# A four-layer transformer kernel rebuilt as one list-scheduled pipeline over token tiles, with the attention scores in packs of four 32-row matmuls

## The chip, the cores and the metric

One core of one Trainium2 chip. The metric is the device time of one execution in microseconds (us). The kernel before takes 821.77 us (median of 3 runs, 820.84 to 821.87). Engines are named as in the profile: PE (TensorE), PEld (its weight loads), DVE (VectorE), ACT (ScalarE), POOL (GpSimd), SP (DMA issue).

The records of TensorE's granted clock show two levels, full and half. The profile gives the mean of the granted clock; this document turns it into "half-clock time" = 2 x (1 - mean clock) x span, the time at half rate that gives that mean. For the kernel before this is 2 x (1 - 0.933) x 818.5 = 110 us. The spacing of matmuls agrees with the records: 512-column matmuls of one stream start every 216 ns where the record says full and every 426 ns where it says half.

## The reference, cut to what matters

S = 2048 tokens, D = 512, 32 heads of 16, a causal window of 256, an MLP of width 1792, bf16. Two layer kinds, each applied twice:

```python
def _A_ref(x, wqkv, wo):                       # H = 32; Dh = 16; W = 256
    q, k, v = ...                              # x @ wqkv, split into heads
    scores = einsum("bhqd,bhkd->bhqk", q, k) * Dh ** -0.5
    mask = (i - j >= 0) & (i - j < W)          # three 128-key blocks per 128 queries
    p = softmax(where(mask, scores, -1e9))
    return einsum("bhqk,bhkd->bhqd", p, v) (heads joined) @ wo

def _B_ref(x, w1, b1, w2, b2):
    return gelu(x @ w1 + b1) @ w2 + b2

x = x + _A_ref(layernorm(x), A_wqkv, A_wo)
x = x + _B_ref(layernorm(x), B_w1, B_b1, B_w2, B_b2)
x = x + _A_ref(layernorm(x), A_wqkv, A_wo)
x = x + _B_ref(layernorm(x), B_w1, B_b1, B_w2, B_b2)
```

The window makes a token tile depend only on itself and the two tiles before it, in every layer. So the four layers can be run as one stream over tiles; nothing forces a layer to end before the next begins.

## The kernel before

It runs layer by layer. `layer_A` normalises all 16 tiles and makes Q, K and V for all of them, then runs attention over 16 tiles; `layer_B` normalises all tiles, then runs the MLP by groups of four tiles. Each `op` goes to its engine's in-order queue in the order in which it is written.

A head has only 16 of the 128 rows of the contraction. The kernel expands K: for each head a copy of 128 rows of K with all rows but that head's 16 set to zero, so that a plain 128-row matmul gives one head's scores.

```python
# K expansion, per tile four multiplies of 128x1024 on VectorE (L614)
op("dve", lambda e, ...: e.tensor_tensor(
    out=KTb[:, sb, kc * HC : (kc + 1) * HC, :],
    in0=KT[:, kc, kcols][:, None, :].to_broadcast([P, HC, P]),
    in1=headmask[:, :, None].to_broadcast([P, HC, P]), op=ALU.mult), ...)

# scores: one 128-row matmul for each head and tile (L638)
op("pe", lambda e, ...: e.matmul(sc[:, ps, hi, 0:N], KTb[:, sb, h, :], QT[:, kc, qcols],
                                 start=True, stop=True), ...)

# exp of two heads (L689); both edges of the band in one VectorE multiply for four heads (L659)
op("act", lambda e, ...: e.activation(Eband[:, eb, h0 : h1 + 1, 0:N], sc[:, ps, :, 0:N], AF.Exp, scale=SCALE), ...)
op("dve", lambda e, ...: e.tensor_tensor(out=Eband[...][:, :, 0:3:2, :], in0=Eband[...][:, :, 0:3:2, :],
                                         in1=mask01[:, None, :, :].to_broadcast([P, nh, 2, P]), op=ALU.mult), ...)

# PV (L710): per head up to three 17-column matmuls (16 values and a sum); then reciprocal,
# normalisation, transposes, output projection, residual, one tile behind
...
# the order of one attention layer
PVLAG = 3
for i, (t, p) in enumerate(jobs):              # tile, pair of heads
    if p in ktb_at: emit_ktb(t + 1, [ktb_at[p]])
    emit_scores(t, p); emit_exp(t, p)
    if p % MASKGRP == MASKGRP - 1: emit_mask(t, p - MASKGRP + 1, p)
    if i >= PVLAG: emit_pv(*jobs[i - PVLAG])
    ...                                        # norm, transposes, output projection of tile t-1
```

LayerNorm's normalisation, its square root and the copies of Q and K out of PSUM run on ScalarE. GpSimd does almost nothing.

The softmax here doesn't subtract the row's maximum and nothing guards it: scores larger than these inputs give would overflow.

## Time and profile before

| | before |
|---|---|
| time, median | 821.77 us |
| span of the profiled execution, mean granted clock | 818.5 us, 0.933 |
| PE / ACT / DVE / POOL busy | 664 / 562 / 471 / 9 us |
| attention, two stretches | 212 + 216 us for 32 tiles: 13.4 us a tile |
| LayerNorm and QKV stretches, four | 68 + 45 + 58 + 46 = 217 us |
| MLP stretches, two | 85 + 89 us |

The page's busy times (share of the span, instructions):

```profile
span 818.5 us, 13174 instructions
...
PE 664.2 (81%) x5728; PEld 362.7 (44%) x5728; DVE 470.9 (58%) x769; ACT 561.6 (69%) x814; POOL 9.3 (1%) x30
```

No engine is full on average. The next view says why: the span in 40 slices, each digit the busy share of a slice in tenths; the last line is the granted clock.

```profile
PE   4996778777778649999979877778787775699998
DVE  5428888888888670222323488887878786401111
ACT  5757888888888476444357488888888884753330
PEclk9998998999999658999989999999999997599999
```

Four stages stand side by side, and twice: where PE is at 9, DVE and ACT are at 1 to 4 (the MLP), and where those are at 8, PE is at 7 (attention). The clock falls in the short stretches between attention and MLP. The table of windows gives the same with numbers. Its columns are the window, its length, the busy time (and count) of PE, PEld, DVE, ACT and POOL, the mean clock, DMA share and GB/s:

```profile
core 0: us, PE busy (x) PEld busy (x) DVE busy (x) ACT busy (x) POOL busy (x), PEclk, DMA share, GB/s
...
68.00:280.00 212.00, 164.94 (x2062) 107.43 (x2063) 172.52 (x248) 179.80 (x254) 0.00 (x0) 0.94 0.01 1
280.00:325.00 45.00, 30.19 (x153) 13.90 (x150) 18.78 (x53) 29.27 (x46) 0.00 (x0) 0.66 0.00 0
325.00:410.00 85.00, 85.00 (x381) 35.74 (x380) 23.31 (x49) 36.59 (x50) 0.00 (x0) 1.00 0.00 1
410.00:468.00 58.00, 51.26 (x270) 24.38 (x268) 17.40 (x33) 36.37 (x58) 2.28 (x1) 0.94 0.00 1
...
```

In attention ACT is busy for 180 and DVE for 173 of 212 us, PE for 165; ACT and DVE wait for each other by way of PE, which is read from the chain below and was not tested. The LayerNorm stretch (280 to 325) uses no engine well and runs PE at clock 0.66. The MLP stretch is bound by PE alone: 85 of 85 us. The chain that ended last, by engine and by line ("issue" is time in which an engine waited for nothing that the profile shows, and a q behind an engine's name marks its sequencer):

```profile
PE 45%; DVE 40%; ACT 14%; issue 1%; POOL 1%; ACTq 0%; POOLq 0%
DVE L_KTb L614 18%; DVE L_Eband L659 12%; PE L_hp L846 12%; PE L_yp L887 12%; ACT L_Eband L689 10%; PE L_pjA L546 6%; PE L_sc L638 4%; PE L_pjA L569 3%; DVE stat L362 3%; PE L_oy L710 3%; DVE X L502 2%; ACT L_xn L439 2%; DVE L_OT_sb L762 1%; PE L_yp L878 1%; DVE statmv L368 1%
```

and the groups that the change touches (line, engine, operation, output and inputs, count; then busy time, mean ns of one, idle time before them and what ended it; "+2 forms" means that the mean mixes three shapes):

```profile
L689 ACT ACTIVATE L_Eband<-L_sc 128x768 bf16<-128x768 f32 (+2 forms) x512 | 363.6, 769 | 72.2 <-PE L_oy L710 61.7
...
L638 PE MATMUL L_sc<-L_QT,L_KTb 128*128 128x384 bf16 (+2 forms) x1024 | 251.7, 332 | 19.7 <-ACT L_Eband L689 10.8
...
L659 DVE TENSOR_TENSOR L_Eband<-L_Eband,mask 128x1024 bf16<-128x1024 bf16 x224 | 151.6, 687 | 64.6 <-ACT L_Eband L689 64.4
...
L614 DVE TENSOR_TENSOR L_KTb<-L_KT,headmask 128x1024 bf16<-128x1024 bf16 x128 | 155.5, 1219 | 0.1
```

The K expansion is a third of DVE's work and 18% of the chain. A score matmul's 332 ns is its length in a pipeline; when scores stand densely in the trace, one starts about every 163 ns (median).

### The profile page before, as it was taken

How to read it: one execution, taken by the hardware profiler on the slowest of the kernel's cores; microseconds unless marked ns; L12 is line 12 of the kernel's file. 1: busy time of each engine (PE TensorE's matmuls, PEld its weight loads, DVE VectorE, ACT ScalarE, POOL GpSimd, SP SyncE). 2: the span in 40 equal slices, each digit the busy share in tenths (PEclk: the TensorE clock that was granted, in tenths of full speed). 3: DMA queues.
4: the chain of work that ended last, by engine and by line, in shares of the span. 5: the costliest groups of instructions: out<-in, count | busy, mean ns of one | idle time of the engine just before them, and what ended most of it. 6: DMA issues, size and time to landing. Idle time of an engine off the chain costs nothing.

```text
span 818.5 us, 13174 instructions
## 1 busy us (share of the span) xinstructions
PE 664.2 (81%) x5728; PEld 362.7 (44%) x5728; DVE 470.9 (58%) x769; ACT 561.6 (69%) x814; POOL 9.3 (1%) x30
## 2 busy tenths in 40 slices
PE   4996778777778649999979877778787775699998
PEld 2442445454555424444435334545454553344443
DVE  5428888888888670222323488887878786401111
ACT  5757888888888476444357488888888884753330
POOL 3000000000000000000010000000000000000000
PEclk9998998999999658999989999999999997599999
DMA  9100000000000000000000000000000000000000
GB/s 339 46 1 0 2 1 2 2 2 2 1 2 1 2 0 1 1 1 1 0 2 1 0 1 2 1 2 1 2 1 2 2 1 2 0 14 19 21 20 33
DMA packets 9675, 10.80 MB, mean 13 GB/s; under 512 B 2193, under 2 KB 8594, under 8 KB 9618
## 3 DMA queue, kind: packets, MB, share of 16 engines
q1 hardware_dynamic: 9618, 9.97, 3.5%
q8 instruction: 45, 0.74, 0.3%
q14 instruction: 12, 0.10, 0.0%
HBM read 7.87 MB, written 2.10 MB: 12 GB/s over the span
## 4 chain that ended last, share of the span: by engine, by line
PE 45%; DVE 40%; ACT 14%; issue 1%; POOL 1%; ACTq 0%; POOLq 0%
DVE L_KTb L614 18%; DVE L_Eband L659 12%; PE L_hp L846 12%; PE L_yp L887 12%; ACT L_Eband L689 10%; PE L_pjA L546 6%; PE L_sc L638 4%; PE L_pjA L569 3%; DVE stat L362 3%; PE L_oy L710 3%; DVE X L502 2%; ACT L_xn L439 2%; DVE L_OT_sb L762 1%; PE L_yp L878 1%; DVE statmv L368 1%
## 5 line engine op out<-in xcount | busy, mean ns | idle before, releaser
L689 ACT ACTIVATE L_Eband<-L_sc 128x768 bf16<-128x768 f32 (+2 forms) x512 | 363.6, 769 | 72.2 <-PE L_oy L710 61.7
L638 PE MATMUL L_sc<-L_QT,L_KTb 128*128 128x384 bf16 (+2 forms) x1024 | 251.7, 332 | 19.7 <-ACT L_Eband L689 10.8
L710 PE MATMUL L_oy<-L_Vaug,L_Eband 128*128 128x17 bf16 x2880 | 180.9, 173 | 83.0 <-DVE L_Eband L659 76.3
L710 PEld LDWEIGHTS L_oy<-L_Vaug,L_Eband 128*128 128x128 bf16 x2880 | 160.3, 99 | 171.5 <-DVE L_Eband L659 99.8
L659 DVE TENSOR_TENSOR L_Eband<-L_Eband,mask 128x1024 bf16<-128x1024 bf16 x224 | 151.6, 687 | 64.6 <-ACT L_Eband L689 64.4
L614 DVE TENSOR_TENSOR L_KTb<-L_KT,headmask 128x1024 bf16<-128x1024 bf16 x128 | 155.5, 1219 | 0.1
L864 ACT ACTIVATE L_gT<-L_hp,b1T 128x512 bf16<-128x512 f32 x112 | 76.0, 687 | 87.3 <-PE L_hp L846 87.2
L502 DVE TENSOR_TENSOR X<-X,L_yp 128x512 bf16<-128x512 bf16 x32 | 22.0, 688 | 176.8 <-PE L_yp L887 176.8
L846 PE MATMUL L_hp<-L_xnT,W_sb 128*128 128x512 bf16 x448 | 105.5, 391 | 1.4 <-ACT L_xnT L474 1.4
L887 PE MATMUL L_yp<-W_sb,L_gT 128*128 128x512 bf16 x448 | 102.3, 380 | 0.0
L638 PEld LDWEIGHTS L_sc<-L_QT,L_KTb 128*128 128x128 bf16 x1024 | 69.7, 98 | 49.0 <-ACT L_Eband L689 25.8
L846 PEld LDWEIGHTS L_hp<-L_xnT,W_sb 128*128 128x128 bf16 x448 | 44.8, 100 | 57.7 <-issue 6.1
L887 PEld LDWEIGHTS L_yp<-W_sb,L_gT 128*128 128x128 bf16 x448 | 41.2, 98 | 52.6 <-issue 7.2
L546 PE MATMUL L_pjA<-L_xnT,Wqkv_sb 128*128 128x512 bf16 x256 | 58.0, 385 | 1.4 <-ACT L_QT L558 1.4
L581 DVE CAST L_Vaug<-L_pjA 128x512 bf16<-128x512 f32 x32 | 22.2, 694 | 61.0 <-PE L_pjA L569 60.8
L774 PE MATMUL L_oy<-Wo_sb,L_OT_sb 128*128 128x512 bf16 x128 | 49.3, 394 | 1.0 <-DVE L_OT_sb L762 1.0
L439 ACT ACTIVATE L_xn<-X,nbias,rstd 128x512 bf16<-128x512 bf16 x64 | 46.7, 803 | 1.8 <-DVE nbias L395 1.8
L362 DVE BATCH_NORM_STATS2 stat<-X 128x6 f32<-128x512 bf16 x64 | 43.1, 673 | 5.4 <-DMA X<-in_A_x_dram 4.8
L452 PE MATMUL L_tpB<-ident,L_xn 128*128 128x128 bf16 x128 | 19.4, 307 | 24.5 <-ACT L_xn L439 15.3
L546 PEld LDWEIGHTS L_pjA<-L_xnT,Wqkv_sb 128*128 128x128 bf16 x256 | 25.2, 100 | 31.4 <-ACT L_QT L558 1.9
L377 ACT ACTIVATE sqv<-statmv,epscol 128x4 f32<-128x4 f32 x16 | 4.8, 297 | 43.0 <-DVE statmv L368 43.0
L558 ACT ACTIVATE L_QT<-L_pjA 128x512 bf16<-128x512 f32 x32 | 18.8, 599 | 15.0 <-PE L_pjA L546 15.0
(45 smaller groups left out, 300.7 us busy)
## 6 DMA issues: line engine op xcount, KB each, us to landing
W_sb<-in_B_w_dram SPq DMA_DIRECT2D x2, 1792.0 KB, 15.4
X<-in_A_x_dram SPq DMA_DIRECT2D x4, 512.0 KB, 6.0
out_dram<-X SPq DMA_DIRECT2D x16, 128.0 KB, 1.7
Wqkv_sb<-in_A_wqkv_dram SPq DMA_DIRECT2D x1, 1536.0 KB, 10.1
Wo_sb<-in_A_wo_dram SPq DMA_DIRECT2D x1, 512.0 KB, 10.6
b1raw<-in_B_b_dram SPq DMA_DIRECT2D x1, 3.5 KB, 15.5
b2row<-in_B_b_dram SPq DMA_DIRECT2D x1, 1.0 KB
```

The costliest lines, as they stand in the source:

```text
L362: lambda e, t=t: e.bn_stats(stat6[:, t, :], X[:, t, :]),
L439: lambda e, t=t, s=s: e.activation(xn[:, s, :], X[:, t, :], AF.Identity, bias=nbias[:, t : t + 1], scale=rstd[:, t : t + 1],),
L546: lambda e, s=s, dc=dc, kc=kc, which=which, cols=cols: e.matmul(pj[:, s, :], Wqkv_sb[:, dc, which * D + kc * P : which * D + (kc + 1) * P] ...
L614: lambda e, sb=sb, kc=kc, kcols=kcols: e.tensor_tensor(out=KTb[:, sb, kc * HC : (kc + 1) * HC, :], in0=KT[:, kc, kcols][:, None, :].to_bro ...
L638: lambda e, ps=ps, hi=hi, sb=sb, h=h, kc=kc, N=N, qcols=qcols: e.matmul(sc[:, ps, hi, 0:N], KTb[:, sb, h, :], QT[:, kc, qcols], start=True ...
L659: lambda e, eb=eb, ha=ha, hb=hb, nh=nh: e.tensor_tensor(out=Eband[:, eb, ha : hb + 1, :].rearrange("p h (b q) -> p h b q", q=P)[:, :, 0:3: ...
L689: lambda e, ps=ps, h0=h0, h1=h1, eb=eb, N=N: e.activation(Eband[:, eb, h0 : h1 + 1, 0:N], sc[:, ps, :, 0:N], AF.Exp, scale=SCALE,),
L710: lambda e, m=m, half=half, col0=col0, eb_k=eb_k, h=h, blk=blk, k=k, kmin=kmin, t=t: e.matmul(oy[:, m, half, col0 : col0 + VW], Eband[:, e ...
L774: lambda e, m=m, c=c: e.matmul(oy[:, m, 1, :], OT_sb[:, c, :], Wo_sb[:, c, :], start=(c == 0), stop=(c == DC - 1)),
L846: lambda e, s=s, dc=dc, fc=fc, cols=cols: e.matmul(hp[:, s, :], W1_sb[:, dc, fc * P : (fc + 1) * P], xnT[:, dc, cols], start=(dc == 0), st ...
L864: lambda e, s=s, fc=fc, gs=gs: e.activation(gT[:, gs, fc, :], hp[:, s, :], AF.Gelu_apprx_tanh, bias=b1T[:, fc : fc + 1], scale=1.0,),
L887: lambda e, ys=ys, gs=gs, fc=fc, ti=ti: e.matmul(yp[:, ys, :], gT[:, gs, fc, ti * P : (ti + 1) * P], W2_sb[:, fc, :], start=False, stop=(f ...
```

## The change

Its intent: no stage stands alone, so that each engine always finds work of some layer; and less work for DVE and ACT in attention. In parts:

1. A planner (`_Plan`) takes every operation with an estimated duration, a priority, its reads and writes and the PSUM banks it takes, simulates the five queues and writes the order in which each engine gets its instructions. The order is fixed when the kernel is built.
2. 32 steps, 16 tiles by two repetitions. Step tau holds the attention of tile tau; QKV is made two pairs of tiles ahead, and the MLP of four tiles is put in behind the attention.
3. Scores: K is written twice when it leaves PSUM, with even heads or odd heads set to zero; a 32-row slice of such a copy holds one head. Four matmuls of 32 rows, one on each 32-row group of the array, form a pack. The K expansion goes.
4. The diagonal edge of the band is masked on DVE, the far edge by a select on GpSimd; LayerNorm's root becomes a power on GpSimd, its normalisation goes to DVE; all copies out of PSUM go to DVE. ACT is left with exp and GELU.
5. Eight PSUM banks: scores take six in rotating sets of four; two ("o") serve PV, transposes, QKV, projections and the second MLP matmul.

The diff has some 1300 lines; this is its core, with cuts marked. Line numbers in the profiles of the changed kernel are those of its own file (L504 is the matmul of `pe_group`, L582 the score pack, L593 and L596 the exps, L600 the mask, L605 the select, L625 PV).

```diff
+    PL = _Plan({"sc": [(0, 1, 2, 3), (4, 5, 0, 1), (2, 3, 4, 5)], "o": [(6,), (7,)],
+                "m1": [(5,), (6,), (7,), (4,), (3,), (2,), (1,), (0,)]})
 ...
+    dma(b1_dma, ["b1raw"], prio=-91)          # planned with the default landing time, 3.0 us
+    add("dve", lambda e, B: e.tensor_copy(b1T[:], b1raw[:]), 100, reads=["b1raw"], writes=["b1T"], prio=-50)
 ...
-    op("dve", ... KTb = KT * headmask ...)    # K expansion, 128 x 128x1024
+    for par in range(2):                      # K out of PSUM, even or odd heads
+        add("dve", lambda e, B, ...: e.tensor_scalar(out=KT[:, kb, par, 2 * i : 2 * i + 2, :],
+            in0=ps[:, B[g][0], :]..., scalar1=parmask[:, par : par + 1], scalar2=None, op0=ALU.mult), ...)
 ...
-    op("pe", ... e.matmul(sc[:, ps, hi, 0:N], KTb[:, sb, h, :], QT[:, kc, qcols]) ...)
+    def sc(e, B, c=c, par=par, gT3=gT3, gS1=gS1):
+        bk = tuple(B[gT3]) + tuple(B[gS1])
+        for r in range(RG):
+            rows = slice(32 * r, 32 * r + 32)
+            x = e.matmul(ps[:, bk[r], 0:N], KT[rows, kb, par, c, kc0 : kc0 + P],
+                         QT[rows, c, t * P : t * P + N], start=True, stop=True)
+        return x
 ...
+    add("dve", ... E[:, es, :, 0:P] *= mask01 ...)                        # diagonal edge
+    if nb == 3:
+        add("pool", lambda e, B, es=es: e.affine_select(                  # far edge
+            E[:, es, :, 2 * P : 3 * P], E[:, es, :, 2 * P : 3 * P], [[0, RG], [-1, P]],
+            ALU.is_ge, 0.0, base=-1, channel_multiplier=1), ...)
 ...
+    def mlp(J, gate_tau, prio1, prio2):
+        gate_pe = (visit_node[(gate_tau, NV - 1)],) if gate_tau < NT else ()
+        gate_act = (exp_last[gate_tau],) if gate_tau < NT else ()
+        for fc in range(FC):
+            pe_group(g, [... W1 ...], 512, 1, xr + ["W1"], prio1 + fc * 0.1, cls="m1", after=gate_pe)
+            gelu_last[0] = add("act", ... Gelu_apprx_tanh ..., after=gate_act)
+        for i in range(4):
+            pe_group(g, [... b2, W2 ...], 512, 1, ..., prio2 + i)
+            residual(tau, 1, g, prio2 + i)
 ...
+    # in attention(): the first exp of a step waits for the last GELU so far
+    if v == 0 and gelu_last[0] is not None:
+        aft = (gelu_last[0],)
 ...
+    qkv(0, -40)
+    qkv(1, -30)
+    for tau in range(NT + BLAG + 1):
+        base = 100.0 * tau
+        if tau % 2 == 0 and tau + 4 < NT:
+            qkv(tau // 2 + 2, base + 120)
+        if tau < NT:
+            attention(tau, base)
+            outproj(tau, base + 130)
+        if tau >= 3 + BLAG and (tau - 3 - BLAG) % 4 == 0:
+            J = (tau - 3 - BLAG) // 4
+            mlp(J, tau, base + 95, base + 250)
```

## The prediction

> **What bounds the kernel now.** It runs four separated stages (timeline, span 818.5 us): LayerNorm+QKV 0-68, attention 68-280, LayerNorm+MLP 280-410, then the same again to 819. PE is busy 664 us, ACT 562, DVE 471 (page), and each stage has its own limit. In attention (2 x about 214 us) ACT is busy 180 of 212 us: the chain of waits gives 40% to DVE (18% K expansion, 12% masking), and ACT waits 62 us in front of exps. In MLP (2 x about 105 us) PE is full at 216 ns per 512-column matmul and ACT and DVE are mostly idle; in the 45 us LayerNorm stretches PE is mostly idle at clock 0.66-0.70.
>
> **What changes.** The main gain is the first.
> - All layers become one pipeline over 32 tile steps, so MLP and QKV matmuls fill PE's gaps under exp.
> - K expansion (128 x 1219 ns, 155 us DVE) goes. PSUM copy with parity mask replaces QK copies: 64 x about 0.7 = 45 us, plus Q copies 22 us, now on DVE instead of ACT.
> - Scores: four K=32 tiles side by side. Before, 1024 matmuls, about 160 ns each when dense (165 us); after, 256 packs. The Trainium skill, "TensorE: Matmul & The Clock Gate", section "Measured speedup vs the span model", gives 3.07x for four row tiles of 512 columns. The skill ("TensorEngine Tiling (Array Packing)", "Key Properties") says a mode change drains PE; estimate 0.4 us per pack with both changes, 100 us.
> - ACT loses normalisation, square roots and all copies (about 110 us). Remaining: exp 364, GELU 76, 16 table loads 20: 460 us.
> - DVE, from measured durations: diagonal masks 256 x 0.42 = 108, stats 55, 64 normalisations about 20, transposed copies 27, K/Q/V 90, reciprocals 256 x about 0.19 = 49, small multiplies 256 x about 0.22 = 56, output copies 13, residuals 44: about 460 us.
> - POOL: 224 selects of 512 elements, from 292 ns for 128: about 0.6 us each, 135 us, plus 128 tiny ops.
> - PE dense: 1184 matmuls of 512 columns 256 us, 512 of 256 columns 56, transposes 22, 2880 PV at about 28 ns (six in 0.16 us in the timeline) 81, scores 100: about 515 us.
>
> **Sum.** Three nearly balanced engines: PE 515, ACT 460, DVE 460. ACT is idle in part of each of 8 GELU phases (56 matmuls 12.1 us, 14 GELUs 9.5). Only two PSUM banks serve PV, projections, transposes and W2; I estimate 12.7 us of holding per step before queueing, against 16.1 of PE. Static order, semaphore latency and these banks should keep the busiest engine near 85%: about 600 us steady, plus about 14 us start and about 20 us end (last MLP alone). Prediction **630 us**, range **575 to 700**. Chances: faster by over 2% 0.96, within 2% 0.02, slower 0.02.
>
> **What would show each step.** Stages gone in the timeline, ACT and DVE busy evenly to the last 25-30 us; ACT about 460, DVE about 460-490, POOL 150-180; PE clock above 0.95; K-expansion group absent; a score pack start to next start 0.3-0.45 us; no engine above about 85% and short waits spread over PE, ACT and DVE, many at PSUM buffers freed by DVE.
>
> **What would make it wrong.** Score packs not overlapping (+70 us PE). POOL selects slowed by DVE masks sharing its SBUF interface ("GPSIMD Engine Reference", "Specifications"; no POOL work overlaps here before), delaying PV. The two PSUM banks queueing worse than thought (towards 700). Small PSUM operations on DVE above 0.2 us.

## The result, and the profile after

The changed kernel is correct and takes **694.28 us** (median of 4 runs, 691.72 to 696.11), beside 821.82 us (820.84 to 822.86) for the kernel before on the same chip. The ratio is 0.8446, with a 95% interval of 0.8416 to 0.8475. Ratios here are the mean time of one kernel's fast runs over that of the other's of the same rounds, so not quite the ratio of the medians quoted. (The first median given for the kernel before is of three of the same four runs.) The prediction was 630 us with a range of 575 to 700: the direction is right, the time lies inside the range but 64 us above the middle.

The page's busy times, then the 40 slices:

```profile
span 694.4 us, 14552 instructions
...
PE 581.8 (84%) x5984; PEld 298.2 (43%) x5984; DVE 423.9 (61%) x1249; ACT 451.9 (65%) x640; POOL 217.4 (31%) x381
```

```profile
PE   0277888898889898899978898898989898799878
...
DVE  0399788837683767838485677837486574625511
ACT  0008798788388836786187955779488964877340
...
PEclk9998687999999888997989999899999998688989
```

The stages are gone from PE's line: 7 to 9 throughout, after two slices of a slow start. But ACT and DVE still dip again and again, ACT to as low as 1. The clock is below full in more places than before, not fewer: 0.906 in the mean, 131 us at half clock against 110.

The windows of start, steady part and tail (columns as before):

```profile
core 0: us, PE busy (x) PEld busy (x) DVE busy (x) ACT busy (x) POOL busy (x), PEclk, DMA share, GB/s
0.00:50.00 50.00, 14.53 (x104) 9.26 (x104) 21.62 (x52) 1.28 (x1) 12.96 (x49) 1.00 0.49 158
50.00:655.00 605.00, 536.45 (x5709) 275.45 (x5708) 394.40 (x1177) 439.05 (x623) 203.62 (x330) 0.90 0.01 4
655.00:694.40 39.40, 30.86 (x176) 13.47 (x176) 7.85 (x22) 11.53 (x17) 0.79 (x2) 0.91 0.05 17
```

This table holds most of the miss. The prediction had 14 us of start, 600 steady and 20 of tail; measured are 50, 605 and 39.4. The chain:

```profile
PE 56%; DVE 27%; ACT 9%; issue 5%; POOL 2%; POOLq 0%; DVEq 0%
PE ps L504 44%; DVE E L600 6%; PE ps L625 5%; ACT E L593 5%; PE ps L582 5%; DVE KT L540 5%; DVE X L513 4%; ACT E L596 3%; DVE stat L470 3%; DVE xn L480 2%; DVE Va L553 2%; DVE Otm L639 2%; PE ps L488 2%; DVE R L636 1%; DVE QT L532 1%
```

and the groups:

```profile
L593 ACT ACTIVATE E<-ps 128x768 bf16<-128x768 f32 (+2 forms) x256 | 198.8, 777 | 197.0 <-PE ps L582 195.2
...
L605 POOL TENSOR_SCALAR_AFFINE_SELECT E<-E 128x512 bf16<-128x512 bf16 x224 | 161.6, 722 | 264.2 <-ACT E L596 263.8
L600 DVE TENSOR_TENSOR E<-E,mask 128x512 bf16<-128x512 bf16 x256 | 123.4, 484 | 20.6 <-ACT E L596 19.7
...
L582 PE MATMUL ps<-QT,KT 32*128 32x384 bf16 (+2 forms) x1024 | 92.3, 350 | 20.3 <-ACT E L593 19.1
```

The K expansion is gone from the chain, and the projections, QKV and MLP (all L504) are now 44% of it. ACT sat idle for 195 us in front of exps, for want of a score pack; before, exps waited 72 us in all. 48 us of that is the start; where most of the rest comes from, windows by step show (a step runs here from one tile's first score pack to the next tile's). The first is a step of attention, QKV and projection alone, the second a burst of the first MLP matmul with its GELUs, the third a step with the second MLP matmul in it:

```profile
105.60:118.70 13.10, 11.21 (x165) 6.12 (x164) 10.94 (x37) 10.96 (x16) 6.62 (x10) 0.70 0.00 1
133.00:147.20 14.20, 14.15 (x104) 6.86 (x104) 3.84 (x11) 11.62 (x16) 0.86 (x1) 0.96 0.00 1
160.90:185.60 24.70, 22.72 (x212) 10.61 (x212) 14.88 (x44) 12.38 (x17) 9.87 (x19) 0.93 0.00 1
```

Eighteen steps without an MLP burst (two of them hold 14 and 17 matmuls of W2) take 13.5 us in the mean (11.9 to 14.9). This is the 13.4 us that one attention tile took before, but it now holds its tile's LayerNorms, QKV and output projection too. Thirteen steps with a burst of W1 or W2 take 26.5 us. So the LayerNorm and QKV stretches were absorbed, and the MLP was not: it stands between steps almost as it stood between layers. The timeline of a W2 burst, PE and then ACT (start, length, operation, count, and in brackets the idle time before it):

```profile
172.98 3.31 PE L504 MATMUL ps<-W_sb,gT 128*128 128x512 bf16 x10
...
179.99 3.20 PE L504 MATMUL ps<-W_sb,gT 128*128 128x512 bf16 x14
183.02 0.45 PE L625 MATMUL ps<-Va,E 128*128 128x17 bf16 x12
183.40 0.34 PE L582 MATMUL ps<-QT,KT 32*128 32x384 bf16 x4
```

```profile
171.61 0.81 ACT L596 ACTIVATE E<-ps 128x768 bf16<-128x768 f32 x1
183.80 0.81 ACT L593 ACTIVATE E<-ps 128x768 bf16<-128x768 f32 x1 [11.38 <-PE ps L582]
```

Ten us of matmuls without one score pack among them, and ACT idle for 11.38 us. W1 bursts are like it, but there the code asks for it: W1 waits for the step's last score pack, GELU for its last exp, and the next step's first exp for the last GELU. Both orders stand in the static queues and could have been read before the run.

The start. The first row is from DVE's queue, the second from PE's:

```profile
27.12 0.17 DVE L460 CAST b1T<-b1raw 128x14 f32<-128x14 bf16 x1 [22.97 <-DMA b1raw<-in_B_b_dram]
...
28.95 0.29 PE L488 MATMUL ps<-ident,xn 128*128 128x128 bf16 x1 [28.95 <-DVE xn L480]
```

A cast of 14 columns, needed only by the first GELU, about 100 us later (the second of the three windows above), stood early in DVE's queue because the planner took its load to land after 3 us. All of LayerNorm after its first instruction stood behind it for 23 us. The Trainium skill ("TensorE: Matmul & The Clock Gate", section "Architectural detail: the array is 16× 32×32, not 1× 128×128") calls the queues of ACT and DVE strictly first-in-first-out, and this trace agrees.

The tail, on PE, after the last score pack at 654.7:

```profile
663.00 0.61 PE L488 MATMUL ps<-ident,xn 128*128 128x128 bf16 x4 [3.21 <-DVE xn L480]
664.12 13.41 PE L504 MATMUL ps<-xnTB,W_sb 128*128 128x512 bf16 x56 [0.52 <-DVE xnTB L493]
```

It is the last tile's PV, projection and LayerNorm (to 664.1), then W1 (13.4 us) and W2 (to 691.3) of the last group with nothing left to run beside them.

### The profile page after: what moved, and what is told of

Same layout as the page of the kernel before. It is cut to its first block, busy times and chain, and to the rows that moved or that the text cites. A ratio compares the mean times of both kernels' runs of the same rounds, so it can differ in the third digit from the quotient of the medians.

```text
span 694.4 us, 14552 instructions
## 1 busy us (share of the span) xinstructions
PE 581.8 (84%) x5984; PEld 298.2 (43%) x5984; DVE 423.9 (61%) x1249; ACT 451.9 (65%) x640; POOL 217.4 (31%) x381
## 4 chain that ended last, share of the span: by engine, by line
PE 56%; DVE 27%; ACT 9%; issue 5%; POOL 2%; POOLq 0%; DVEq 0%
PE ps L504 44%; DVE E L600 6%; PE ps L625 5%; ACT E L593 5%; PE ps L582 5%; DVE KT L540 5%; DVE X L513 4%; ACT E L596 3%; DVE stat L470 3%; DVE xn L480 2%; DVE Va L553 2%; DVE Otm L639 2%; PE ps L488 2%; DVE R L636 1%; DVE QT L532 1%
## 5 line engine op out<-in xcount | busy, mean ns | idle before, releaser
L593 ACT ACTIVATE E<-ps 128x768 bf16<-128x768 f32 (+2 forms) x256 | 198.8, 777 | 197.0 <-PE ps L582 195.2
L605 POOL TENSOR_SCALAR_AFFINE_SELECT E<-E 128x512 bf16<-128x512 bf16 x224 | 161.6, 722 | 264.2 <-ACT E L596 263.8
L596 ACT ACTIVATE E<-ps 128x768 bf16<-128x768 f32 (+2 forms) x256 | 199.0, 777 | 0.0
L625 PE MATMUL ps<-Va,E 128*128 128x17 bf16 x2880 | 112.4, 173 | 32.1 <-DVE Otm L639 7.7
L600 DVE TENSOR_TENSOR E<-E,mask 128x512 bf16<-128x512 bf16 x256 | 123.4, 484 | 20.6 <-ACT E L596 19.7
L625 PEld LDWEIGHTS ps<-Va,E 128*128 128x128 bf16 x2880 | 95.0, 98 | 86.5 <-issue 30.3
L504 PE MATMUL ps<-W_sb,gT 128*128 128x512 bf16 x448 | 113.8, 396 | 0.0
L582 PE MATMUL ps<-QT,KT 32*128 32x384 bf16 (+2 forms) x1024 | 92.3, 350 | 20.3 <-ACT E L593 19.1
L504 PE MATMUL ps<-xnTB,W_sb 128*128 128x512 bf16 x448 | 104.2, 388 | 0.5 <-DVE xnTB L493 0.5
L684 ACT ACTIVATE gT<-ps,b1T 128x512 bf16<-128x512 f32 x112 | 76.4, 687 | 28.4 <-PE ps L504 28.0
L504 PE MATMUL ps<-xnTA,Wqkv_sb 128*128 128x256 bf16 x512 | 84.3, 311 | 7.4 <-DVE KT L540 4.9
L474 POOL TENSOR_SCALAR veps<-statmv 128x1 f32<-128x1 f32 x64 | 14.9, 233 | 174.4 <-DVE statmv L472 174.0
L504 PEld LDWEIGHTS ps<-xnTB,W_sb 128*128 128x128 bf16 x448 | 42.9, 99 | 50.0 <-issue 3.5
L504 PEld LDWEIGHTS ps<-W_sb,gT 128*128 128x128 bf16 x448 | 40.9, 100 | 53.4 <-issue 15.4
L504 PEld LDWEIGHTS ps<-xnTA,Wqkv_sb 128*128 128x128 bf16 x512 | 49.2, 108 | 26.7 <-DVE KT L540 7.1
L663 DVE COPY OT<-ps 128x512 bf16<-128x512 bf16 x32 | 13.4, 419 | 73.9 <-PE ps L658 73.3
L582 PEld LDWEIGHTS ps<-QT,KT 32*128 32x128 bf16 x1024 | 26.3, 93 | 74.4 <-ACT E L593 46.7
L636 DVE RECIPROCAL R<-ps 128x4 f32<-128x4 f32 x256 | 44.6, 174 | 14.6 <-PE ps L625 13.6
L540 DVE TENSOR_SCALAR KT<-ps,parmask 128x512 bf16<-128x512 f32 x64 | 46.3, 738 | 4.4 <-PE ps L504 4.1
```

What stands on the lines that cost most here:

```text
L504: r = e.matmul(ps[:, B[g][0], cols], lhsT, rhs, start=st, stop=sp)
L540: kn = (add("dve", lambda e, B, g=g, i=i, par=par: e.tensor_scalar(out=KT[:, kb, par, 2 * i : 2 * i + 2, :], in0=ps[:, B[g][0], :].rearran ...
L582: x = e.matmul(ps[:, bk[r], 0:N], KT[rows, kb, par, c, kc0 : kc0 + P], QT[rows, c, t * P : t * P + N], start=True, stop=True)
L593: a = add("act", lambda e, B, gT3=gT3, es=es: e.activation(E[:, es, 0:2, 0:N], ps[:, B[gT3][0] : B[gT3][0] + 2, 0:N], AF.Exp, scale=SCALE) ...
L596: a2 = add("act", lambda e, B, gS1=gS1, es=es: e.activation(E[:, es, 2:4, 0:N], ps[:, B[gS1][0] : B[gS1][0] + 2, 0:N], AF.Exp, scale=SCALE ...
L600: add("dve", lambda e, B, es=es: e.tensor_tensor(out=E[:, es, :, 0:P], in0=E[:, es, :, 0:P], in1=mask01[:, None, :].to_broadcast([P, RG, P ...
```

## The experiments

Letters in the expectations name theories, which each text states. "Correct" is against the reference; three kernels are wrong. Three of the kernels had one run each that was slow (the fifth, seventh and ninth); ratios leave it out, the medians in the table do not.

| kernel | median us | ratio to before | half-clock us (profiled run) |
|---|---|---|---|
| changed | 694.28 | 0.8446 | 131 |
| e1_b1_late | 679.35 | 0.8265 | 141 |
| e2_w2_spread | 673.74 | 0.8215 | 106 |
| e3_staged | 719.73 | 0.8771 | 208 |
| e4_filler | 685.87 | 0.8347 | 64 |
| e5_b1_last | 669.80 | 0.8126 | 103 |
| e6_full_rows | 714.54 | 0.8699 | 10 |
| e7_no_select | 670.76 | 0.8136 | 113 (slow run) |
| e8_combined | 656.35 | 0.7991 | 140 |
| e9_select_aside | 688.94 | 0.8373 | 107 |
| e10_dve_masks | 723.66 | 0.8816 | 226 |
| e11_comb_filler | 645.91 | 0.7853 | 47 |
| e12_third_bank | 702.63 | 0.8562 | 147 |

Where a difference to the changed kernel is given in us below, it is the difference of the medians of fast runs (for the three kernels with a slow run these are 668.33, 669.98 and 687.12 us); the changed kernel was measured in another session, so the ratios, each taken beside the same kernel before, are the sounder comparison.

### The start: e1_b1_late and e5_b1_last

```diff
-        add("dve", lambda e, B: e.tensor_copy(b1T[:], b1raw[:]), 100, reads=["b1raw"], writes=["b1T"], prio=-50)
+        add("dve", lambda e, B: e.tensor_copy(b1T[:], b1raw[:]), 100, reads=["b1raw"], writes=["b1T"], prio=200)
```

> One edit: the cast of the MLP bias b1 gets a late place in VectorE's order instead of the second. Theory H: in the changed kernel VectorE sits 23.0 us at the start in front of this cast, for the last but one of the input DMAs, and everything behind it in the queue waits too; the first score pack should then start near 28 us instead of 49.9, nothing else should move, and the time fall by about 21 us, to 668 to 678 us. Rival: the start is held by the input DMAs of the weights as such (the DMA queues are busy to about 27 us); then the first score pack stays past 40 us and the time falls by less than 8 us.

Correct, 679.35 us (677.91 to 679.78). The first score pack came at 37.6 us instead of 49.9, and 15 us were gained, not the 21 expected. The trace says why: a wait of 10.16 us for the same load remained. The planner fills an idle queue with whatever it holds ready, so a lower priority moved the cast only a little. The edit was not strong enough to judge the theory by, so the next one changes what the planner believes:

```diff
-        dma(b1_dma, ["b1raw"], prio=-91)
+        dma(b1_dma, ["b1raw"], prio=-91, dur=60000.0)
```

> The first run only moved the b1 cast a little later in VectorE's order, and a wait of 10.2 us for the same DMA stayed. Here the planner is told that this DMA lands at 60 us, so the cast stands behind some 130 VectorE instructions. Theory H: no wait for an input DMA over 2 us is left on VectorE, the first score pack starts at 26 to 30 us and the time is 667 to 675 us, about 22 us under the changed kernel. Rival: once the cast is out of the way the start is held by something else (the other input DMAs, the chain of LayerNorm and K copies on VectorE): the first score pack stays past 34 us, the time at 677 or more.

Correct, 669.80 us (662.46 to 674.92). The first score pack, in PE's timeline:

```profile
26.60 0.34 PE L582 MATMUL ps<-QT,KT 32*128 32x384 bf16 x4
```

23.3 us earlier than in the changed kernel (49.9), and 26 us gained: one misjudged load was worth 3.7% of the kernel. It also leaves 26.6 us of a start for which 14 had been predicted, so the prediction was wrong there without the cast too. The fastest of its runs is the one with the highest clock (0.922).

### Is the MLP under the exps? e3_staged

The planner is kept, but the MLP of a repetition is put after its last attention step (and the second repetition's QKV after that):

```diff
-        for tau in range(NT + BLAG + 1):
-            ...
-            if tau >= 3 + BLAG and (tau - 3 - BLAG) % 4 == 0:
-                J = (tau - 3 - BLAG) // 4
-                mlp(J, tau, base + 95, base + 250)
+        for rep in range(NREP):
+            ...                                # QKV, attention and outproj of the repetition's 16 tiles
+            for J in range(rep * (T // 4), (rep + 1) * (T // 4)):
+                base = 3000.0 * rep + 1700.0 + 100.0 * (J % (T // 4))
+                mlp(J, (rep + 1) * T - 1, base, base + 50)
```

> The same pipeline, score packs, tiles and helper functions, but the MLP groups of a repetition are added after its last attention step and gated by it, so that no MLP matmul runs during attention: the overlap of MLP with attention is undone, the overlap of LayerNorm, QKV and output projection with the exps is kept. Theory N: in the changed kernel the MLP runs as bursts during which no exp runs, so its overlap is worth little: this kernel takes 680 to 725 us. Rival O (the prediction's): filling PE's gaps under the exps with the MLP is the main gain: this kernel takes over 750 us.

Correct, 719.73 us (718.38 to 723.96). Interleaving the MLP with attention is worth 0.8771 / 0.8446 = 1.038, or 25 us; over 750 us, which the expectation laid down for the prediction's "main gain", is refuted. Of the 127 us that the change gains, 102 are there with the MLP standing apart as before. Much of the 25 may be clock: the staged kernel is at half clock for 208 us, 77 more than the changed one, and its first attention stretch has a mean clock of 0.78. If the 0.28 us of time for each us at half clock that is found below among runs of one kernel held between kernels too (not shown), 77 us would stand for 22 of the 25.

### W2 as a burst or spread: e2_w2_spread

Each W2 tile's matmuls get priorities that rise by 6, so that they lie between the visits (score packs) of one step, one tile of the group in each of four steps. The edit also lets W2 begin in the step right after its W1, one step sooner than before (105 in place of 250), so it moves the burst as well as spreading it:

```diff
-        def pe_group(g, mms, dur, step, reads, prio, cls="o", after=(), fresh=True):
+        def pe_group(g, mms, dur, step, reads, prio, cls="o", after=(), fresh=True, pstep=0.0):
 ...
-                add("pe", fn, len(part) * mm(dur), reads=rd, writes=["ps:" + g], prio=prio,
+                add("pe", fn, len(part) * mm(dur), reads=rd, writes=["ps:" + g], prio=prio + pstep * (i // step),
 ...
-                    ... for fc in range(FC)], prio2 + i)
-                residual(tau, 1, g, prio2 + i)
+                    ... for fc in range(FC)], prio2 + 100 * i, pstep=6.0)
+                residual(tau, 1, g, prio2 + 100 * i + 80)
-                mlp(J, tau, base + 95, base + 250)
+                mlp(J, tau, base + 95, base + 105)
```

> One edit: the priorities of the W2 matmuls, so that one output tile's 15 matmuls are spread between the score packs of the attention steps instead of running mostly as one burst of about 10 us without a score pack. Theory W: the bursts starve ScalarE (195 us of waits in front of exps), and W2 fits under the exps; then the steps of 24 to 28 us with a W2 burst shrink, ScalarE's waits in front of exps fall by 40 us or more, the half-clock time falls, and the time falls by 30 to 70 us, to 625 to 665. Rival B: a W2 tile that is spread holds one of only two PSUM banks for the whole step, so PV, projections and transposes queue for the other: then the attention steps lengthen and the time stays within 2% or rises. Rival P: PE itself bounds the steady stretch, so its order does not matter: within 2%, with PE busy time unchanged.

Correct, 673.74 us (671.66 to 680.05), 2.7% under the changed kernel (0.8215 / 0.8446), between the two expectations. ACT's idle time in front of exps fell from 197.0 to 155.6 us (the line names only the first releaser, the score packs, with 122.4; the trace puts another 30.5 us down to the PV matmuls, L625):

```profile
L593 ACT ACTIVATE E<-ps 128x768 bf16<-128x768 f32 (+2 forms) x256 | 199.5, 779 | 155.6 <-PE ps L582 122.4
```

Two windows, a step with a part of W2 in it and a step with W1:

```profile
143.80:157.50 13.70, 12.59 (x132) 5.46 (x134) 8.41 (x27) 13.00 (x18) 6.66 (x11) 1.00 0.01 2
...
186.50:217.60 31.10, 28.39 (x276) 15.13 (x280) 17.66 (x52) 21.57 (x30) 8.20 (x13) 0.97 0.01 2
```

The first of them holds 25 recorded W2 matmuls and is no longer than a step without any: here W2 does fit under the exps, which in bursts of 24.7 us a step it did not. Steps with a part of W2 and no W1 take 12 to 17 us. But the steps with W1 grew to between 28 and 35 us, most of them with 39 or 40 recorded QKV matmuls in place of 24 to 28 and some 13 of W2 besides. So the burst does cost time, and the new order gives part of the gain back elsewhere.

### The two shared banks: e12_third_bank

```diff
-            "o": [(6,), (7,)],
+            "o": [(6,), (7,), (5,)],
```

> One edit to the changed kernel: the pool that serves PV, projections, transposes and W2 may take a third PSUM bank, one of the six of the score packs, when the other two are taken; the planner orders everything anew. Theory B (in the prediction): two banks for all of that queue, and PE waits for VectorE to free them; the time falls by 10 us or more, to under 685. Rival S: the bank is missing where a score pack needs four of six, so the exps wait more; the time rises by 10 us or more. Neither: within 1.5% of 694.

Correct, 702.63 us (701.70 to 703.60): 0.8562 against 0.8446, 1.4% slower: the third of the outcomes laid down, within 1.5%. ACT's wait in front of exps stayed at 195 us, and the clock is lower (0.895). Bank 5 also belongs to the scores, so the edit takes from them what it gives. The prediction's fear of two queueing banks is not supported by this run; it isn't excluded either, since all eight banks that the kernel has are in use and none could be added.

### The clock: e4_filler and e6_full_rows

PE was never idle for more than 1.06 us within the steady part, yet the clock was at half for 131 us. The theory under test: the grant follows the share of time in which columns stream through the array, and short matmuls with waits between (PV: 17 columns; packs: four matmuls in the time of one) leave that share low. e4 adds a useless matmul of 255 columns before each PV group, into columns of that group's bank that nobody reads. The planner isn't told of it, so the order of all other instructions is the same:

```diff
                 def pvm(e, B):
+                    e.matmul(ps[:, B[g][0], 128:383], E[:, eslot(tau - t + kmin, v), 0, (t - kmin) * P : (t - kmin + 1) * P],
+                             Va[:, (tau - t + kmin) % VR, 0:15, :].rearrange("p h d -> p (h d)"), start=True, stop=True)
                     for r in range(RG):
```

> One useless matmul of 255 columns is added in front of each of the 256 groups of PV matmuls, into an unused part of the same PSUM bank; the order of everything else is unchanged. It adds about 256 x 0.11 = 27 us to PE at full clock. In the two traces a 3.4 us window of PE's clock record in which the array streams under about 0.4 of the time is followed by one at half clock; the changed kernel has 132 us of half clock. Theory C: the half clock costs about 30 us and the filler lifts most windows over that line: half-clock time falls below 50 us and the time stays within 1.5% or falls. Rival P: PE is the bound and the clock follows something else: half-clock time stays above 100 us and the time rises by 25 to 35 us. Rival A: PE's work in the attention steps is hidden under the exps: half clock falls and the time does not move.

Correct, 685.87 us (683.45 to 687.41): 1.2% faster with 256 matmuls more, a small difference, but the two intervals of the ratio (0.8322 to 0.8373 and 0.8416 to 0.8475) don't touch. The clock by slices:

```profile
PEclk9999998999999999999999999999999999789989
```

Against the line of the changed kernel the dips in the middle are gone: half-clock time 64 us instead of 131 (under 50 had been expected). The filler's own work is about 256 x 255 / 512 x 216 ns = 28 us, an estimate from the 216 ns of a 512-column matmul. So a clock that was only partly mended gained 8 us net; how much of the 28 us it had to pay back first, and how much of them lay in PE's waits and cost nothing, this run doesn't tell.

e6 gives the packs back their full 128 rows (and so wrong scores), which puts four matmuls one after the other where the pack had them side by side:

```diff
-                        rows = slice(32 * r, 32 * r + 32)
+                        rows = slice(0, P)
```

> Wrong result on purpose: each of the four score matmuls of a pack takes all 128 rows instead of its own 32, so the four run one after the other; the order, the banks and all other engines' work are unchanged. Row packing alone is undone. Theory R: four matmuls in a row cost 4 x 160 ns against about 340 to 370 for the pack, 0.27 us x 224 = 60 us of PE, part of it hidden under exps and paid back by a higher clock (the array streams more): half-clock time under 60 us, time 705 to 745 us. Rival: the packs save PE time that PE was not short of, and the half clock that they bring takes it back: 685 to 702 us.

714.54 us (714.01 to 714.74), and the steadiest of all kernels. Its clock:

```profile
PEclk9999999999999999999999999999999999999979
```

Ten us at half clock. The pack of four took 824 ns from first start to last end, against 342, and about 660 ns of PE's time against about 370 for the row pack with a mode change (from the full array to row groups, and back) on both sides. The row packing, which by these figures takes some 256 x 0.29 = 74 us of work off PE (an estimate at full clock), brought a net 20 us (0.8699 against 0.8446). The rest went to the clock, or was never on the critical path; these two are not told apart.

The clock records change level only at multiples of 3.413 us. Windows of that length laid over the traces of the kernels before and after agree with this reading: after a full-clock window in which the array streamed for less than 0.35 of the time, the next window was at half clock in 18 of 19 cases in the changed kernel and 7 of 7 in the one before; above 0.45 it never was (109 and 154 cases); between, it was in 7 of 27 and 7 of 41. Over the traces of all fourteen kernels the counts are 185 of 196 and 0 of 1736. PE's busy share separates less well: below 0.7 it was followed by half clock in 13 of 20 and in 14 of 43 windows. That is read from traces, with streaming counted as 512 columns in 216 ns and a row pack counted once; only e4 and e6 test it. Among repeated runs of one kernel the time follows the clock too: over the 45 fast runs of the twelve experiments, each compared with the mean of its kernel, 1 us more at half clock goes with 0.28 us more time (correlation 0.84). That is no proof of a direction.

### Masks: e7_no_select, e9_select_aside and e10_dve_masks

e7 cuts the select to one column (wrong):

```diff
-                        E[:, es, :, 2 * P : 3 * P], E[:, es, :, 2 * P : 3 * P], [[0, RG], [-1, P]],
+                        E[:, es, :, 2 * P : 2 * P + 1], E[:, es, :, 2 * P : 2 * P + 1], [[0, RG], [-1, 1]],
```

> Wrong result on purpose: the 224 tail selects on GpSimd work on one column per head in place of 128, so GpSimd's work in the attention steps nearly goes; the order is unchanged. In the changed kernel the diagonal mask on VectorE takes 484 ns on average where the same form took 421 before, and the select 722 ns. Theory S: the two engines slow each other at SBUF, but neither is what PE waits for: the masks fall to 420 to 430 ns, VectorE's busy time by 10 to 20 us, the time by less than 1.5% (684 to 695). Rival: the selects delay PV: the time falls by over 15 us.

670.76 us (663.07 to 673.54; 669.98 in fast runs), 24 us less. The effect that theory S named is there, but larger than it said, and of the size that its rival had named. The profiled run was slow, so only lengths of instructions on other engines than PE are taken from it: the mask on DVE fell from 484 to 416 ns in the mean:

```profile
L600 DVE TENSOR_TENSOR E<-E,mask 128x512 bf16<-128x512 bf16 x256 | 105.9, 416 | 23.1 <-ACT E L596 21.2
```

and DVE's busy time from 423.9 to 401.8 us: the select cost DVE 22 us. The changed kernel's trace shows how. Of its 256 masks, 89 overlap no select and take 413 ns in the mean. 82 begin before a select; they take 421, and that select 845 instead of 635. 85 begin while a select runs, and these take 619 ns: 66 of them end 273 to 277 ns after the select does, however early in it they began. (Of the other 19, 6 began within a few tens of ns of the select and won, the rest met only its end.) So whichever comes second is held until the first is through. LayerNorm's normalisations on DVE show the same (405 ns alone, 623 behind a select), its statistics (L470) and the copies of K out of PSUM (L540) do not. The two held groups add up to 85 x 206 + 29 x 218 ns = 24 us, about the 22 measured. Is the gain DVE's, or does PV wait less for the select? e9 keeps the select and its load on GpSimd, but lets it write a tile that nobody reads, so that PV doesn't wait for it (wrong; the order of all instructions is the same):

```diff
+        aside = sb("aside", [P, 2, RG, P])
-                        E[:, es, :, 2 * P : 3 * P], E[:, es, :, 2 * P : 3 * P], [[0, RG], [-1, P]],
+                        aside[:, es % 2, :, :], E[:, es, :, 2 * P : 3 * P], [[0, RG], [-1, P]],
```

> Wrong result on purpose: GpSimd does the same 224 tail selects of 512 elements, at the same places of its order, but writes them into a tile aside that nobody reads, so PV no longer waits for them; the order on every engine is that of the changed kernel. It parts the two ways in which the selects can have cost the 23 us that went with them in the run before. Theory D: they slow VectorE at SBUF (masks 484 against 416 ns, normalisations 502 against 406), and VectorE, in its strict order, passes that on to PE: masks stay near 480 ns and the time stays at 686 to 697 us. Rival L: PV waits for the select's own latency (the profile puts only 6.7 us of PE's waits down to it, but a wait for several is put down to the last): the time falls to 668 to 680 us although the masks stay slow.

688.94 us (685.27 to 696.73; 687.12 in fast runs), only 7 us less, with the masks as slow as in the changed kernel:

```profile
L601 DVE TENSOR_TENSOR E<-E,mask 128x512 bf16<-128x512 bf16 x256 | 122.6, 481 | 20.6 <-ACT E L597 19.4
```

So of e7's 24 us about 17 are DVE held up by the select, and 7 are waits of PV for it (20 and 6 by the ratios). A rival, that LayerNorm's power waits behind the selects in GpSimd's queue, finds no support: DVE's normalisations waited 11.1 us for it in the changed kernel, 10.6 in e7 and 11.6 in e9. Some of the 17 may have come by way of the clock, which was 0.923 to 0.935 in e7's fast runs against 0.906 to 0.915. e10 asks whether the select should be there at all. It masks both edges in one DVE multiply, as the kernel before did:

```diff
-                add("dve", ... E[:, es, :, 0:P] *= mask01 ..., d_bf2(4 * P), ...)
-                    add("pool", ... affine_select ...)
+                    add("dve", lambda e, B, es=es: e.tensor_tensor(
+                        out=E[:, es, :, :].rearrange("p h (b q) -> p h b q", q=P)[:, :, 0:3:2, :],
+                        in0=E[:, es, :, :].rearrange("p h (b q) -> p h b q", q=P)[:, :, 0:3:2, :],
+                        in1=mask2[:, None, :, :].to_broadcast([P, RG, 2, P]), op=ALU.mult), d_bf2(8 * P), ...)
```

> The other way round, with a right result: the tail select goes back from GpSimd to VectorE, as one multiply of 1024 elements for both blocks, 687 ns in the kernel before. VectorE gains about 224 x (0.687 - 0.484) = 45 us, less 6 us for normalisations that run undisturbed: busy about 460 us. Theory V: VectorE's pace sets that of the attention steps (as the run without selects suggests), so each of the 32 steps lengthens by about 1 us: 700 to 730 us. Rival L: only the select's latency counted, and VectorE has room: 670 to 690 us.

Correct, 723.66 us (721.75 to 727.47), 29 us slower. DVE has 457 us of work instead of 424, and the clock, at 0.844, is the lowest of all:

```profile
PEclk9995586987989789897959879996998989569979
```

The move to GpSimd is a gain of 29 us, with its interference paid; how much of the 29 is the lower clock isn't told apart.

### What points to a better kernel: e8_combined and e11_comb_filler

e8 is e5 and e2 together; e11 adds e4's filler. The diffs are those shown.

> The b1 cast out of the way and W2 spread between the score packs, together; the result is right. If the two gains are of different places (the start, the steady stretch) they add: 694 - 22 - 20 = 652, range 645 to 660 us. If the spread's gain had come from the same place as the other, 665 or more.

Correct, 656.35 us (654.24 to 658.24). The two gains add for the greater part: 26.0 + 20.5 = 46.5 by the medians, 38 found; the clock (0.893) is lower than in either.

> The combined version (656 us) with the filler matmul of the fourth run. The combined version still has 140 us at half clock. If the clock is again what it costs, half-clock time falls below 70 us and the time by 5 to 12 us, to 644 to 652; if PE, busier here than in the changed kernel, cannot hide 27 us more of matmuls, the time rises above 660.

Correct, **645.91 us** (641.03 to 647.38): the best version found, 0.7853 / 0.8446 = 0.930 of the changed kernel. Its busy times and its clock:

```profile
PE 576.5 (90%) x6240; PEld 311.0 (49%) x6240; DVE 420.1 (66%) x1249; ACT 455.7 (71%) x640; POOL 218.6 (34%) x381
...
PEclk9998899999899997998899998999989999799999
```

With 47 us at half clock instead of e8's 140, it is 10 us faster with an estimated 28 us more to do on PE: the filler helps again.

## Why the prediction was right or wrong

The time fell in the range, and the outcome given a chance of 0.96 came about. The middle was 64 us too low, and one central reason was wrong, so that part of the agreement is luck.

**Where the 64 us are** (from the windows): start +36 (50 against 14), steady part +5 (605 against 600), tail +19 (39.4 against 20); the sum of the prediction's terms, 634, had been rounded to 630.

- **Start, the term "about 14 us start".** 23 us of the 36 is the cast of b1 waiting for its load in DVE's queue (e5, shown). The rest is a mis-sized term: loads, LayerNorm and two QKV pairs take 26.6 us to the first pack even so.
- **Tail, the term "about 20 us end (last MLP alone)".** The last group's LayerNorm chain (9 us after the last pack), W1 (13.4) and W2 (13.6) follow one another.
- **Steady part, the term "about 600 us".** The size held, by errors that offset each other, which is luck: PE's "about 515 us" measured 582, because 118 us of its busy time fell into half-clock time (with half of that taken off it is 523, an estimate), while PE was at 89% of the steady part (536 of 605) instead of 85%. The step that failed is "MLP and QKV matmuls fill PE's gaps under exp", called the main gain. QKV does, MLP does not: W1 and W2 run as bursts of about 10 us with ACT idle, and interleaving them is worth 25 us, the effect on the clock included (e3). PE's share was as high as predicted without the overlap, since bursts are dense for PE; the busiest engine's share said nothing about who overlaps with whom.
- **"PE clock above 0.95"** was wrong: 0.906. The prediction took the half-clock time of the kernel before to belong to its LayerNorm stretches, which go. In their place came packs and short PV matmuls, too thin to hold the clock. Filling them halves the half-clock time (e4) and is worth 8 us net of the filler's own cost.
- **Score packs.** The estimate of 0.4 us a pack with both changes was right: 342 ns in length, and about 370 ns of PE's time with both mode changes. The quoted 3.07 was not what arrived: 4 x 160 to 163 ns, about 650, over 370 is 1.75. The Trainium skill's "Mode switching requires drain" ("TensorEngine Tiling (Array Packing)", "Key Properties") agrees with the trace: the start of a pack came 312 ns after the 512-column matmul before it, against 216 for another such matmul, 96 ns more.
- **ACT about 460 us** right (452); **DVE 460 to 490** too high (424), with masks slower than reckoned and several small groups shorter (reciprocal 174 ns, small multiply 220); **POOL 150 to 180** wrong (217): the select took 722 ns in the mean, not 600, and the power of 128 single values 585 ns each, 37 us.
- **The risk named first to last.** "Packs not overlapping" did not happen. "POOL selects slowed by DVE masks sharing its interface" did, in both directions: a mask that came first made its select 845 ns long instead of 635, but the select also slows DVE, and that is worth more, 17 to 20 us (e7, e9); its wait in PV is 6 to 7 us. The page named in the prediction, "GPSIMD Engine Reference", "Specifications", says that VectorE instructions with two SBUF inputs contend with GpSimd, and this trace agrees (the masks that met a running select: 619 ns against 413). "Two PSUM banks queueing" found no support (e12).

**Where the 127 us come from.** Shown by runs: 102 are there without any MLP interleaving (e3). Row packing is worth 20 (e6), and the far mask on GpSimd 29 (e10); these were measured one at a time from the changed kernel and need not add. Read from the traces only: 217 us of separate LayerNorm and QKV stretches were taken into attention steps whose length didn't change, 13.4 before and 13.5 after, which was possible because 155 us of K expansion left DVE and some 110 us of copies and normalisation left ACT. No run puts the K expansion back alone, so its own share stays open.

## What to carry to other kernels

Before counting on overlap, read in the queues' order which instruction follows which: a planner that held a stage behind a gate, or gave it one priority, made a burst here, however balanced the busy totals look. A planner's order is as good as its guesses of when loads land, because one tiny operation waiting at the head of an in-order queue holds everything behind it (here 23 us). And taking work off the tensor engine can lower its clock (131 us at half clock with row packs, 10 with full rows in e6), so a saving there has to be checked against the granted clock before it is booked.

## What the Trainium skill lacked or had wrong

- "TensorE: Matmul & The Clock Gate", sections "What's actually happening" and "HAM oscillation — how this bites in real kernels": the rule is put as no idle gap over about 3.4 us. Here PE was never idle over 1.06 us in the steady part, and 131 us ran at half clock. What went with it was the streaming share of a window of 3.413 us: below 0.35 mostly half clock next (18 of 19), above 0.45 never (0 of 109). The section on queue cycling ("A second HAM failure mode: psum-queue depth-cycling") tells of the effect of small idles, without a threshold. A filler matmul cut the half-clock time to 64 us (e4).
- The same page, "Measured speedup vs the span model": 3.07 for four row tiles of 512 columns; here about 1.75 for 384 columns in a stream mixed with full-array matmuls. The starts within a pack, 0, 3, 7 and 10 ns, agree with its 4 ns per tile.
- "TensorEngine Tiling (Array Packing)", "Key Properties": a mode change drains the engine, with no cost given. Here 96 ns on entering a pack.
- "GPSIMD Engine Reference", "Specifications" (and "SBUF — State Buffer", "Who interferes with whom", which says that the later one blocks fully): the trace agrees with both: a mask that began during a select ended 273 to 277 ns after it. No size for a mixed stream is given. Here the mask went from 416 to 484 ns in the mean and up to 867, the select to 722 from a median of 635, and the kernel lost 17 to 20 us.
- No page that was consulted gives the length of a power on GpSimd: 585 ns for 128x1.
